# A fused attention and routed-FFN kernel: VectorE's small operations taken from a list, one behind each two-bank maximum

## The chip, the cores and the metric

One core of a Trainium2 chip runs the whole kernel in one launch. The metric is the device time of that launch in microseconds (us). Engines are called TensorE (PE in the profile, its weight loads PEld), VectorE (DVE), ScalarE (ACT), GpSimd (POOL) and SyncE (SP); SP issues most of the DMAs.

## What is computed

The reference takes x (2048 tokens of 512 features) and mixes two branches with a gate per token. Branch a is softmax attention with 32 heads of 16 features. Branch b routes only the two tokens with the highest router score through a SwiGLU feed-forward net; all others pass unchanged.

```python
g = sigmoid((x * gate_w).sum(-1, keepdims=True))
# branch a: 32 heads, Dh = 16
p = softmax(einsum("bhqd,bhkd->bhqk", q, k) * Dh ** -0.5)
a = einsum("bhqk,bhkd->bhqd", p, v) ... @ wo
# branch b: r = x @ w_r; idx = the two largest of r
y = (silu(x_sel @ w_gate) * (x_sel @ w_up)) @ w_down
y = y * sigmoid(r[idx])
b = x + scatter(y at idx)
out = g * a + (1 - g) * b
```

## The kernel before

The attention is cut into 32 units (a pair of heads and half of the queries; the last four are cut otherwise), each of 16 steps (one tile of 128 keys). Everything runs in the order in which the program is written: each engine takes its instructions in that order, and the loops at the end of the function interleave several streams by hand.

Three streams make up the main phase. The **m stream** (`m_piece`, L563) computes scores with queries on the partitions only to find the row maxima of the softmax: 64 matmuls of 512 keys for a unit. Three pieces make a period: two matmuls into the two banks of the tile `mxa`, one into the bank `mxb`. VectorE reduces `mxa` in one instruction (the **two-bank maximum**) and `mxb` in another (the **one-bank maximum**), both at L577, with a minus sign, into `Mr`. The **s stream** (`s_piece`, L634) computes the scores again with keys on the partitions, and ScalarE takes their exponential (L642) into `P`; the negative maximum is in the query operand as two more rows (48 and 49 of each half), so that the exponential needs no bias. The **A stream** (`av_mm`, L644) multiplies `P` with V; a column of ones gives the softmax denominators. The s stream trails the m stream by 21 steps.

The string `ORDER` (L30) sets how they interleave: a round is twelve s, twelve m, three A and one `f`, that is three steps and four periods. `f` is a fill: a quarter of a projection of a later head group, a part of the feed-forward net or of the output projection (`slots`, L800). Work with a due step is entered with `at_step(s, f, ...)` and called by `end_step(s)`, right behind the fourth s piece of step s, wherever VectorE's stream stands then.

Besides the maxima VectorE has small operations:

- the **minimum** (`m_unit`, L614, instruction at L616): when a unit's 64 pieces are reduced, the four partial (negative) maxima of each row are combined. GpSimd then splits the result in a high and a low part (`pool_split`, L75 to L77).
- the **turning** (`m_rows`, L624, instruction at L627): a transpose of 32x32 blocks of the split values, followed by eight DMAs on SP that put them into the two rows of the query tile. The list `turn` holds it together with a count; each maximum takes one off, and at zero, three maxima after the minimum, it is issued.
- the **reciprocals of the denominators** (`l_out`, L691, instruction at L694): eight of 16 columns after every eighth unit, one at the end of each of eight successive steps; the eighth stores them to DRAM on SP.
- the **router**: `route_rows` (L334) takes the eight largest of 16 rows of 128 scores and their places, `route_best` (L344) the eight largest of the 128 candidates; their results go through DMAs on SP. `route_index` and `gather` (L350, L354) fetch the two tokens with indirect DMAs of GpSimd; at the end of `gather` the router's sigmoid is computed, an exponential on ScalarE, "+1" and reciprocal on VectorE. `x_rows` (L362) is the first that uses the fetched tokens.
- the reciprocals of the gates (`gates`, L320) and of the feed-forward's SiLU (`ff_h`, L416).

Of the kernel before, what the change touches and what calls it, by code (L numbers as in the profile page):

```python
# [1 line left out]

# [8 lines left out]
AF = mybir.ActivationFunctionType  # L11
OP = mybir.AluOpType
# [7 lines left out]
UNITS = PAIRS * 2  # L20
# [4 lines left out]
EL = 64  # L25
# [10 lines left out]
def gated_mix(ctx: ExitStack, tc: tile.TileContext, xT, x, wqkv, wo, w_rg, w_gate, w_up, w_down,  # L36
              consts, pos, out):
    nc = tc.nc
# [49 lines left out]
    top8 = cp.tile([16, 8], F32, name="top8")  # L88
    idx8 = cp.tile([16, 8], U32, name="idx8")
    num8 = cp.tile([16, 8], F32, name="num8")  # L90
    cand = cp.tile([1, 128], F32, name="cand")
    best8 = cp.tile([1, 8], F32, name="best8")
# [4 lines left out]
    rsel = cp.tile([2, 1], F32, name="rsel")  # L97
# [202 lines left out]
    rg = {}  # L300
# [32 lines left out]

    def route_rows():  # L334

        nc.vector.max(top8, rg["row"])
        nc.vector.max_index(idx8, top8, rg["row"])
        nc.gpsimd.tensor_copy(num8, idx8)
        nc.gpsimd.tensor_scalar(num8, num8, row0[:16], None, op0=OP.add)
        nc.gpsimd.tensor_copy(idx8, num8)  # L340
        nc.sync.dma_start(cand, top8)
        nc.sync.dma_start(ap(i_scr, 0, [[8, 16], [1, 8]]), idx8)

    def route_best():  # L344
        nc.vector.max(best8, cand)
        nc.vector.max_index(pos8, best8, cand)
        nc.sync.dma_start(pos2, pos8[:, 0:2])
        nc.sync.dma_start(rsel, best8[:, 0:2])
# [5 lines left out]
    def gather():  # L354
        nc.gpsimd.indirect_dma_start(out=xsel, out_offset=None, in_=x,
                                     in_offset=bass.IndirectOffsetOnAxis(ap=idx2[:, :1], axis=0))
        nc.gpsimd.memset(xselT, 0.0)
        nc.scalar.activation(rsel, rsel, AF.Exp, scale=-1.0)
        nc.vector.tensor_scalar(rsel, rsel, 1.0, None, op0=OP.add)
        nc.vector.reciprocal(rsel, rsel)  # L360

    def x_rows():  # L362
        ps = fl_tile((128, 4, 2))
# [199 lines left out]
    def m_piece(g):  # L563

        u, e = divmod(g, EL)
        t, c, j = e // 8, e // 2 % 4, e % 2
        r = g % 3
        if r == 0:
            MX[0] = mxa_tile()
        elif r == 2:  # L570
            MX[1] = mxb_tile()
        dst = MX[0][:, r] if r < 2 else MX[1]
        nc.tensor.matmul(dst, Qx[u % 3][64 * j:64 * j + 48, t * 128:t * 128 + 128],  # L573
                         k_of(u, t // 4)[64 * j:64 * j + 48, c * 512:c * 512 + 512], start=True, stop=True)
        if r:
            g0 = (g - 1 if r == 1 else g) % (3 * EL)
            nc.vector.tensor_reduce(Mr[:, g0:g0 + (2 if r == 1 else 1)], MX[r - 1], axis=AX.X, op=OP.max, negate=True)  # L577
            if turn:
                turn[0][0] -= 1
            if e == EL - 1 or (e == 0 and r == 1 and g):  # L580
                m_unit(u if e else u - 1)
            if turn and turn[0][0] <= 0:
                m_rows(*turn.pop()[1:])

    def m_lead(n):

        if n < 16:
            u, t, c = 0, n // 8 * 4 + n % 4, n // 4 % 2 * 2
        else:
            u, t, c = 1, (n - 16) // 2, n % 2 * 2  # L590
        for i in range(3):
            if i == 0:
                tl = mxa_tile()
                dst = [tl[:, 0], tl[:, 1]]
            else:
                tl = (mxb_tile, fl_tile, av_tile)[(2 * n + i) % 3]()
                dst = [tl]
            for k, d in enumerate(dst):
                j, cc = (k, c) if i == 0 else (i - 1, c + 1)
                nc.tensor.matmul(d, Qx[u][64 * j:64 * j + 48, t * 128:t * 128 + 128],  # L600
                                 Kx[0][64 * j:64 * j + 48, cc * 512:cc * 512 + 512], start=True, stop=True)
            o = EL * u + t * 8 + (c * 2 if i == 0 else c * 2 + 1 + i)
            reds.append((Mr[:, o:o + len(dst)], tl))
        for r in reds:
            nc.vector.tensor_reduce(*r, axis=AX.X, op=OP.max, negate=True)  # L605
        reds.clear()
        if n == 15:
            m_unit(0)
        elif n == 16:
            m_rows(*turn.pop()[1:])  # L610

    reds = []

    def m_unit(u):  # L614
        m = ring.tile([128, 2, 8], F32, tag="m", name="m", bufs=2)
        nc.vector.tensor_reduce(m, Mr[:, EL * (u % 3):EL * (u % 3) + EL].rearrange("p (t c j) -> p j t c", c=4, j=2),  # L616
                                axis=AX.X, op=OP.min)
        hl = ring.tile([128, 2, 2, 8], F32R, tag="hl", name="hl", bufs=2)
        pool_split(hl[:, :, 0], hl[:, :, 1], m)
        turn.append([3 if u < UNITS - 1 else 0, u, hl])  # L620

    turn = []

    def m_rows(u, hl):  # L624

        r = ring.tile([128, 32], F32R, tag="hr", name="hr", bufs=2)
        nc.vector.transpose(r.bitcast(F32), hl.rearrange("p j i t -> p (j i t)").bitcast(F32))  # L627
        for j in range(2):
            for b in range(4):
                q = Qx[u % 3][64 * j + 48:64 * j + 50, :].rearrange("i (t n) -> i t n", n=128)  # L630
                p0 = 32 * b + 16 * j
                nc.sync.dma_start(q[:, :, 32 * b:32 * b + 32].bitcast(F32), r[p0:p0 + 16, :].bitcast(F32))
# [130 lines left out]
    fill, now = {}, [0]  # L763

    def at_step(s, f, *a):
        fill.setdefault(s, []).append((f, a))
# [11 lines left out]
        at_step(-19 + t, products, t)  # L778
    at_step(-1, r_row)
    at_step(1, gates, 0)  # L780
    at_step(2, route_rows)
    at_step(4, gates, 1)
    at_step(10, route_best)
    at_step(16, route_index)
    at_step(22, gather)
    at_step(-8, load_w, 1)
    at_step(-5, split_w, 1)
    at_step(2, load_w, 2)
# [11 lines left out]
    def slots():  # L800
        for w, nb in order:
            yield from proj(1, w, nb, 3)
        late.append((split_w, (2,)))
        at_step(now[0] + 4, load_w, 3)
        x_rows()
        yield
        for w, nb in order:
            yield from proj(2, w, nb, 3)
        for n, (w, nb) in enumerate(order):
            yield from proj(3, w, nb, 3)  # L810
            if w == "q":
                for i in range(4):
                    at_step(now[0] + i + 1, load_ff, ("gate", "up")[i // 2], (w_gate, w_up)[i // 2],
                            ("xh", "xl")[i // 2], nb, i % 2)
        yield from ff_in("gate")
        for j in range(4):
            at_step(now[0] + 2 * j, load_down, j)
        ff_t(0, "gate")
        yield
        yield from ff_in("up")  # L820
        ff_t(1, "up")
        late.append((ff_act, ()))
        at_step(now[0] + 3, ff_h)
        at_step(now[0] + 3, load_wo)
        for c in range(4):
            at_step(now[0] + 6 + c, split_wo, c)
        yield
        yield
        yield from ff_down()
        ff_sum()  # L830
        last_tiles()
        s = now[0]
        for nb in range(4):
            at_step(s + 5 + 2 * nb, load_acc, nb)
        for t in range(16):
            at_step(s + 11 + t, acc_scale, t)
        at_step(s + 1, load_at, 0, (0, 1))
        at_step(s + 4, split_at, 0, (0, 1))
        yield from wait(s + 8)
        yield from wo_groups((0, 1), (2,))  # L840
        assert now[0] > 3 * 8 * KT + 16
        yield from wo_groups((2,))
        for t in range(12, 16):
            wo_last(t, 64)
            yield
        for t in range(12):
            if t % 4 == 0:
                yield from wait((478, 494, 505)[t // 4])
            wo_last(t, 128)
            yield  # L850

    fills = slots()
# [5 lines left out]
    def p_v(s):  # L858
        if not 0 <= s < STEPS:
            return  # L860
        av_mm(s)
        if s % KT < KT - 1:
            return
        u, s = s // KT, now[0]
        av_out(u)
        if u % 8 == 7 and u < 24:
            for i in range(8):
                at_step(s + 6 + i, l_out, u // 8, i)
        elif u == QU - 1:
            for i in range(8):  # L870
                at_step(s + 6 + i, l_out, 3, i)
            for i in range(4):
                at_step(s + 16 + 2 * i, l_last, i // 2, i % 2)
                at_step(s + 19 + 2 * i, n_last, i // 2, i % 2)
            at_step(s + 27, split_last, 3)
        elif QU <= u < UNITS - 1:
            at_step(s + 3, l_unit, u, 0)
            at_step(s + 6, l_unit, u, 1)
            at_step(s + (13 if u == QU else 7), split_last, u - QU)
# [59 lines left out]
        next(fills, None)  # L939
        end_step(s)  # L940
    end_step(STEPS + 2)
    assert next(parts, 0) == 0 and not fill and next(fills, 0) == 0, fill
    tail()


# [29 lines left out]
```

## Time and profile before

| what | value |
|---|---|
| device time, median of 3 runs | 1437.01 us (1435.02 to 1437.27) |
| device time of the profiled execution | 1437.04 us |
| its span, first to last instruction | 1435.2 us |
| TensorE busy | 1423.6 us (99%) |
| VectorE busy | 1295.4 us (90%), 1535 instructions |
| ScalarE busy | 1169.7 us (82%) |
| GpSimd busy | 312.0 us (22%) |
| two-bank maxima (L577) | 655, mean 1213 ns |
| one-bank maxima (L577) | 654, mean 691 ns |

A row of a group reads: line, engine, operation, output and input tiles with their shapes, count, busy time and mean of one, and behind the second bar the idle time of the engine just ahead of these instructions and what ended most of it. A row of a timeline reads: start, duration, engine, line, operation, tiles, and in brackets the idle time ahead and what ended it. Matmuls are pipelined and the ends of their rows are modelled, so their starts are the better measure.

### The profile page before, as it was taken

The numbers are of one execution on the slowest core, as the hardware profiler recorded it, in microseconds if no ns is written. First come the engines' busy times: TensorE is split into PE (matmuls) and PEld (weight loads), VectorE is DVE, ScalarE is ACT, GpSimd is POOL, SyncE is SP. The second block draws the span as 40 slices with busy tenths as digits, with TensorE's granted clock in tenths as the row PEclk, the third lists the DMA queues.
The fourth block names the chain that finished last, engine by engine and source line by source line (L and its number), as shares of the span: only waits on it lengthen the run. The fifth ranks groups of instructions, "written<-read, shape, count | busy, mean of one in ns | idle before, by whom it ended". The sixth has DMA issues, their size and how long they took to land.

```text
span 1435.2 us, 24154 instructions
## 1 busy us (share of the span) xinstructions
PE 1423.6 (99%) x9113; PEld 630.2 (44%) x9113; DVE 1295.4 (90%) x1535; ACT 1169.7 (82%) x2262; POOL 312.0 (22%) x328
## 2 busy tenths in 40 slices
PE   9999999999999999999999999999999999999998
PEld 6654444444444444444444444344444444444433
DVE  5879999999999999999999999999999999999942
ACT  4568888888888888888888888888888888888885
POOL 3652000112000001200000100032742322234500
PEclk9999999999999999999999999999999999999998
DMA  8612021212214121312222332414313031012012
GB/s 266 185 33 63 20 53 31 53 45 40 54 50 112 62 53 30 68 29 57 65 82 53 87 87 73 108 41 128 82 31 68 23 75 37 13 30 58 16 50 77
DMA packets 55096, 92.87 MB, mean 65 GB/s; under 512 B 14208, under 2 KB 25472, under 8 KB 53476
## 3 DMA queue, kind: packets, MB, share of 16 engines
q1 hardware_dynamic: 54884, 91.32, 24.3%
q8 instruction: 72, 1.18, 0.4%
q14 instruction: 44, 0.36, 0.1%
q0 software_dynamic: 96, 0.01, 0.0%
HBM read 63.77 MB, written 28.57 MB: 64 GB/s over the span
## 4 chain that ended last, share of the span: by engine, by line
PE 96%; DMA 2%; DVE 1%; ACT 0%; SPq 0%; issue 0%; ACTq 0%; DVEq 0%
PE av L650 35%; PE st L641 23%; PE mxa L573 12%; PE mxb L573 10%; PE fl L153 6%; PE fl L495 4%; PE st L282 3%; DMA xs<-xT 1%; PE mxa L600 1%; DMA wvs<-wqkv 1%; PE fl L386 0%; PE st L153 0%; DVE Mr L577 0%; DMA k_scr<-Qx 0%; ACT P L642 0%; PE fl L424 0%
## 5 line engine op out<-in xcount | busy, mean ns | idle before, releaser
L642 ACT ACTIVATE P<-st 128x512 f32<-128x512 f32 x2028 | 1064.5, 599 | 204.2 <-PE st L641 102.3
L577 DVE TENSOR_REDUCE Mr<-mxa 128x2 f32<-128x1024 f32 x655 | 794.4, 1213 | 4.0 <-PE mxa L573 3.5
L650 PE MATMUL av<-P,V 128*32 128x512 f32 x4096 | 545.3, 604 | 0.0
L641 PE MATMUL st<-Qx,Kx 50*128 50x512 f32 x2028 | 537.8, 443 | 1.8 <-ACT P L642 1.7
L577 DVE TENSOR_REDUCE Mr<-mxb 128x1 f32<-128x512 f32 x654 | 451.8, 691 | 63.5 <-PE st L641 18.6
L641 PEld LDWEIGHTS st<-Qx,Kx 50*128 50x128 f32 x2028 | 275.3, 184 | 232.7 <-ACT P L642 213.0
L573 PE MATMUL mxb<-Kx,Qx 48*128 48x512 f32 x654 | 325.4, 498 | 0.0
L573 PE MATMUL mxa<-Kx,Qx 48*128 48x512 f32 x1310 | 296.9, 420 | 1.2 <-DVE Mr L577 1.2
L573 PEld LDWEIGHTS mxb<-Kx,Qx 48*128 48x128 f32 x654 | 119.5, 183 | 273.7 <-DVE Mr L577 251.9
L573 PEld LDWEIGHTS mxa<-Kx,Qx 48*128 48x128 f32 x1310 | 124.9, 183 | 52.1 <-DVE Mr L577 9.9
L650 PEld LDWEIGHTS av<-P,V 128*32 128x32 f32 x4096 | 81.1, 108 | 140.6 <-issue 134.5
L189 POOL TENSOR_SCALAR ev<-pe 128x512 fp32r<-128x512 f32 x24 | 35.7, 1489 | 321.5 <-ACT pe L187 321.5
L76 POOL TENSOR_SCALAR hl<-m 128x16 fp32r<-128x16 f32 x32 | 8.1, 254 | 440.0 <-DVE m L616 440.0
L462 POOL TENSOR_TENSOR acc<-acc,w 128x512 f32<-128x512 f32 x32 | 41.0, 1280 | 166.9 <-ACT w L461 152.8
L153 PE MATMUL fl<-xh,wh 128*128 128x512 f32 x96 | 42.9, 447 | 0.0
L153 PE MATMUL fl<-xh,wl 128*128 128x512 f32 x96 | 40.4, 420 | 0.0
L546 DVE SCALAR_TENSOR_TENSOR acc<-fl,gg,acc 128x512 f32<-128x512 f32 x16 | 12.0, 748 | 26.3 <-PE fl L495 24.0
L495 PE MATMUL fl<-woh,ahl 128*128 128x512 f32 x96 | 35.2, 447 | 0.0
L605 DVE TENSOR_REDUCE Mr<-mxa 128x2 f32<-128x1024 f32 x21 | 25.7, 1222 | 8.3 <-PE mxa L600 8.3
L153 PE MATMUL fl<-xl,wh 128*128 128x512 f32 x96 | 32.6, 421 | 0.0
L190 POOL TENSOR_TENSOR ev<-pe,ev 128x512 fp32r<-128x512 f32 x24 | 30.8, 1283 | 2.0
L282 PE MATMUL st<-Kx,xh 128*128 128x512 f32 x64 | 28.1, 440 | 0.0
(173 smaller groups left out, 763.0 us busy)
## 6 DMA issues: line engine op xcount, KB each, us to landing
Kx<-k_scr SPq DMA_DIRECT2D x30, 256.0 KB
k_scr<-ev SPq DMA_DIRECT2D x14, 512.0 KB
q_scr<-ev SPq DMA_DIRECT2D x14, 512.0 KB
Qx<-q_scr SPq DMA_DIRECT2D x54, 128.0 KB
Qx<-q_scr SPq DMA_DIRECT2D x70, 64.0 KB
xs<-xT SPq DMA_DIRECT2D x16, 256.0 KB
xn<-x SPq DMA_DIRECT2D x4, 1024.0 KB
Qx<-hr SPq DMA_DIRECT2D x256, 2.0 KB
```

Source lines behind the costliest of these rows:

```text
L153: nc.tensor.matmul(ps, a[:, i, c, :], b[nb][:, c, :], start=n == 0, stop=n == 11)
L189: nc.gpsimd.tensor_scalar(ev[:, 0], t, 1.0, None, op0=OP.mult)
L190: nc.gpsimd.tensor_sub(ev[:, 1], t, ev[:, 0].bitcast(F32))
L282: nc.tensor.matmul(ps, a[nb][:, c, sl], b[:, c, :], start=c == 0 and n == 0, stop=c == 3 and n == 2)
L462: nc.gpsimd.tensor_add(a, a, w)
L495: nc.tensor.matmul(ps, a[:, sl], b[:a.shape[0], c, :], start=first and n == 0, stop=last and n == 2)
L573: nc.tensor.matmul(dst, Qx[u % 3][64 * j:64 * j + 48, t * 128:t * 128 + 128], k_of(u, t // 4)[64 * j:64 * j + 48, c * 512:c * 512 + 512], ...
L577: nc.vector.tensor_reduce(Mr[:, g0:g0 + (2 if r == 1 else 1)], MX[r - 1], axis=AX.X, op=OP.max, negate=True)
L605: nc.vector.tensor_reduce(*r, axis=AX.X, op=OP.max, negate=True)
L641: nc.tensor.matmul(ps, k, q, start=True, stop=True)
L642: nc.scalar.activation(P[s][:, 2 * j + c, :], ps, AF.Exp)
L650: nc.tensor.matmul(AV[0][32 * ct:32 * ct + 32, :], V[:, kt, h * VW:h * VW + 32], P[s][:, ct, :], start=kt == 0, stop=kt == KT - 1)
```

## The change

A list `gaps` holds closures. In `m_piece`, directly behind a two-bank maximum (r == 1), a pending turning is issued if there is one; otherwise, if the piece isn't among the first two or the last of its unit, the oldest entry of `gaps` is called. So at most one of them follows each two-bank maximum. The count in `turn` is gone: the turning of a unit follows the first two-bank maximum after its minimum. `m_unit`, which issues the minimum, is called where it was: behind a two-bank maximum in two of three units, behind a one-bank maximum in the third.

The denominators' reciprocals, the router's two pairs, the gates' reciprocal and `ff_h` no longer run at the end of a step but are appended to `gaps` there. Each of the router's pairs is taken apart, the MAX8 one entry and the rest another. Some due steps are later by one or two (`route_best` 10 to 12, `route_index` 16 to 18, `gather` 22 to 24). The router's sigmoid becomes a function of its own: the exponential stays at step 22, its "+1" goes from VectorE to GpSimd, and its reciprocal is appended at step 27.

```diff
@@ route_rows, route_best, gather
-        nc.vector.max(top8, rg["row"])
         nc.vector.max_index(idx8, top8, rg["row"])
-        nc.vector.max(best8, cand)
         nc.vector.max_index(pos8, best8, cand)
-        nc.scalar.activation(rsel, rsel, AF.Exp, scale=-1.0)
-        nc.vector.tensor_scalar(rsel, rsel, 1.0, None, op0=OP.add)
-        nc.vector.reciprocal(rsel, rsel)
+    def route_gate(i):
+        if i == 0:
+            nc.scalar.activation(rsel, rsel, AF.Exp, scale=-1.0)
+            nc.gpsimd.tensor_scalar(rsel, rsel, 1.0, None, op0=OP.add)
+        else:
+            nc.vector.reciprocal(rsel, rsel)
@@ m_piece
             nc.vector.tensor_reduce(Mr[:, g0:g0 + (2 if r == 1 else 1)], MX[r - 1], axis=AX.X, op=OP.max, negate=True)
-            if turn:
-                turn[0][0] -= 1
+            if r == 1:
+                if turn:
+                    m_rows(*turn.pop())
+                elif e > 1 and e < EL - 1 and gaps:
+                    gaps.pop(0)()
             if e == EL - 1 or (e == 0 and r == 1 and g):
                 m_unit(u if e else u - 1)
-            if turn and turn[0][0] <= 0:
-                m_rows(*turn.pop()[1:])
+                if u == UNITS - 1 and e:
+                    m_rows(*turn.pop())
@@ m_unit
-        turn.append([3 if u < UNITS - 1 else 0, u, hl])
+        turn.append((u, hl))
-    turn = []
+    turn, gaps = [], []
@@ due steps
-    at_step(2, route_rows)
-    at_step(4, gates, 1)
-    at_step(10, route_best)
-    at_step(16, route_index)
-    at_step(22, gather)
+    at_step(2, gaps.append, lambda: nc.vector.max(top8, rg["row"]))
+    at_step(3, gaps.append, route_rows)
+    at_step(4, gaps.append, partial(gates, 1))
+    at_step(10, gaps.append, lambda: nc.vector.max(best8, cand))
+    at_step(12, gaps.append, route_best)
+    at_step(18, route_index)
+    at_step(22, route_gate, 0)
+    at_step(24, gather)
+    at_step(27, gaps.append, partial(route_gate, 1))
-        at_step(now[0] + 3, ff_h)
+        at_step(now[0] + 3, gaps.append, ff_h)
-                at_step(s + 6 + i, l_out, u // 8, i)
+                at_step(s + 6 + i, gaps.append, partial(l_out, u // 8, i))
-                at_step(s + 6 + i, l_out, 3, i)
+                at_step(s + 6 + i, gaps.append, partial(l_out, 3, i))
```

More of the change, by code (lines that the diff above doesn't have):

```diff
@@ L1 @@
 from contextlib import ExitStack
+from functools import partial
 import concourse.bass as bass
@@ L609, in m_lead @@
         elif n == 16:
-            m_rows(*turn.pop()[1:])
+            m_rows(*turn.pop())
     reds = []
@@ L941, in gated_mix @@
     end_step(STEPS + 2)
-    assert next(parts, 0) == 0 and not fill and next(fills, 0) == 0, fill
+    assert next(parts, 0) == 0 and not gaps and not fill and next(fills, 0) == 0, fill
     tail()
```

## The prediction

> **What bounds the kernel now.** I read the page first (busy time, chain), then the groups by line, the waits, and last the timeline of VectorE and of TensorE, one engine at a time, because the change only shifts VectorE's small operations by a few instructions.
>
> ```profile
> span 1435.2 us, 24154 instructions
> ...
> PE 1423.6 (99%) x9113; PEld 630.2 (44%) x9113; DVE 1295.4 (90%) x1535; ACT 1169.7 (82%) x2262; POOL 312.0 (22%) x328
> ...
> PE 96%; DMA 2%; DVE 1%; ACT 0%; SPq 0%; issue 0%; ACTq 0%; DVEq 0%
> ...
> L577 DVE TENSOR_REDUCE Mr<-mxa 128x2 f32<-128x1024 f32 x655 | 794.4, 1213 | 4.0 <-PE mxa L573 3.5
> ...
> L577 DVE TENSOR_REDUCE Mr<-mxb 128x1 f32<-128x512 f32 x654 | 451.8, 691 | 63.5 <-PE st L641 18.6
> ```
>
> TensorE is busy for 1423.6 us of 1435.2 and has 96% of the chain that ended last; VectorE follows at 90%. A two-bank and a one-bank maximum take 1213 + 691 = 1904 ns together, so VectorE has little room in a period (one of each). Ahead of a two-bank maximum it idles 4.0 us in all, ahead of a one-bank maximum 63.5 us, or 97 ns each: VectorE's spare time lies behind the two-bank maximum. Four undisturbed periods show both engines:
>
> ```profile
> 402.91 1.21 DVE L577 TENSOR_REDUCE Mr<-mxa 128x2 f32<-128x1024 f32 x1
> 404.22 0.69 DVE L577 TENSOR_REDUCE Mr<-mxb 128x1 f32<-128x512 f32 x1
> 404.83 1.22 DVE L577 TENSOR_REDUCE Mr<-mxa 128x2 f32<-128x1024 f32 x1
> 406.16 0.69 DVE L577 TENSOR_REDUCE Mr<-mxb 128x1 f32<-128x512 f32 x1
> 406.76 1.22 DVE L577 TENSOR_REDUCE Mr<-mxa 128x2 f32<-128x1024 f32 x1
> 408.00 0.69 DVE L577 TENSOR_REDUCE Mr<-mxb 128x1 f32<-128x512 f32 x1
> 408.61 1.22 DVE L577 TENSOR_REDUCE Mr<-mxa 128x2 f32<-128x1024 f32 x1
> 410.02 0.69 DVE L577 TENSOR_REDUCE Mr<-mxb 128x1 f32<-128x512 f32 x1 [0.20 <-PE st L641]
> ```
> ```profile
> 404.24 0.46 PE L573 MATMUL mxa<-Kx,Qx 48*128 48x512 f32 x2
> ...
> 406.19 0.41 PE L573 MATMUL mxa<-Kx,Qx 48*128 48x512 f32 x2
> ...
> 408.04 0.52 PE L573 MATMUL mxa<-Kx,Qx 48*128 48x512 f32 x2
> ...
> 410.06 0.39 PE L573 MATMUL mxa<-Kx,Qx 48*128 48x512 f32 x2
> ```
>
> A period is about 1.9 us (402.91, 404.83, 406.76, 408.61). From a one-bank maximum to the two-bank one is 0.61 us, back to back. From a two-bank to the next one-bank maximum it is 1.31, 1.33, 1.24 and 1.41 us, mean 1.32: the last part is waiting for TensorE. The two-bank maxima end at 404.12, 406.05, 407.98 and 409.83, and the score matmuls that overwrite their banks start 0.12, 0.14, 0.06 and 0.23 us later. Where TensorE really waits (below), it starts about 0.06 us after the end, so the **slack** of a two-bank maximum is 0.06, 0.08, 0 and 0.17 us, mean 0.08. Whatever delays it by more stops TensorE, and TensorE is the chain. A delay of a one-bank maximum first eats up the gap in front of it.
>
> **The change part by part.** It removes one operation of VectorE and moves the others. The matmuls keep their order, and so do ScalarE's activations.
>
> *Router.* Three groups stand behind one-bank maxima today.
>
> ```profile
> 104.41 0.27 DVE L336 MAX8 top<-rt 16x8 f32<-16x128 f32 x1
> 104.71 0.08 DVE L337 MATCH_VALUE_LOAD idx<-top,rt 16x8 f32 x1
> ...
> 104.99 1.19 DVE L577 TENSOR_REDUCE Mr<-mxa 128x2 f32<-128x1024 f32 x1
> ```
> ```profile
> 106.24 0.50 PE L573 MATMUL mxa<-Kx,Qx 48*128 48x512 f32 x2 [0.35 <-DVE Mr L577]
> ```
> ```profile
> 126.20 0.27 DVE L345 MAX8 best<-cand 1x8 f32<-1x128 f32 x1
> ...
> 126.78 1.19 DVE L577 TENSOR_REDUCE Mr<-mxa 128x2 f32<-128x1024 f32 x1
> ```
> ```profile
> 128.08 0.50 PE L573 MATMUL mxa<-Kx,Qx 48*128 48x512 f32 x2 [0.33 <-DVE Mr L577]
> ```
> ```profile
> 157.15 0.69 DVE L577 TENSOR_REDUCE Mr<-mxb 128x1 f32<-128x512 f32 x1
> 158.37 0.14 DVE L359 TENSOR_SCALAR rsel<-rsel 2x1 f32<-2x1 f32 x1 [0.53 <-ACT rsel L358]
> ...
> 158.62 1.19 DVE L577 TENSOR_REDUCE Mr<-mxa 128x2 f32<-128x1024 f32 x1
> ```
> ```profile
> 159.87 0.50 PE L573 MATMUL mxa<-Kx,Qx 48*128 48x512 f32 x2 [0.51 <-DVE Mr L577]
> ```
>
> At 104.41 stood a MAX8 and a FIND_INDEX8 (with its value load). Without them the two-bank maximum would have ended at 104.41 + 1.21 = 105.62; it ended at 104.99 + 1.19 = 106.18, 0.56 us late, and TensorE shows 0.35 us idle, ended by that maximum. The same pair at 126.20: end at 127.97 instead of 127.41, 0.56 late, 0.33 idle. At 158.37 VectorE waited 0.53 us for ScalarE's exponential and then ran two tiny operations: the maximum ended at 159.81 instead of 157.15 + 0.61 + 1.21 = 158.97, 0.84 late, 0.51 idle. The visible idle, 0.35 + 0.33 + 0.51 = 1.19 us, is a lower bound, the whole delay, 1.96 us, an upper one. I take delay less mean slack: 0.48 + 0.48 + 0.76 = **1.72 us**.
>
> What is late next: MAX8, FIND_INDEX8 and the reciprocals now stand singly in gaps. From FIND_INDEX8's load to the next maximum is 104.99 - 104.71 = 0.28 us; in a gap it would start 1.13 us after the two-bank maximum (shown below), and 1.13 + 0.28 = 1.41 is 0.09 more than the mean gap, against 0.08 of slack: nothing, twice. The "+1" of the router's gate goes to GpSimd, which is idle then; ScalarE is no longer waited for by VectorE, since the reciprocal is queued five steps later. On SP, two weight loads now go ahead of the candidates' store, and eight row loads ahead of the store of the positions: a few microseconds, while TensorE first uses the gathered rows at 352.3 us, so I cost this at nothing.
>
> ```profile
> L365 PE MATMUL fl<-cst,xsel x4: 196/197/218, 352.3 to 352.5; 2*128 2x2 f32 x4
> ```
>
> Were that cover gone, VectorE's second MAX8 would wait for the candidates. Elsewhere on SP one feed-forward weight load changes places with a store of denominators, also far from its use.
>
> *Softmax denominators.* Of 32 reciprocals (4 bursts of 8), by the order of VectorE's instructions, 21 stand behind a one-bank maximum and 11 behind a two-bank one; all 32 go into gaps.
>
> ```profile
> L627 DVE STREAM_TRANSPOSE hr<-hl 128x32 f32<-128x32 f32 x32 | 6.4, 201 | 0.7 <-POOL hl L77 0.7
> L694 DVE RECIPROCAL Lt<-Lt 128x16 f32<-128x16 f32 x24 | 5.8, 241 | 0.0
> ```
> ```profile
> 780.71 0.24 DVE L694 RECIPROCAL Lt<-Lt 128x16 f32<-128x16 f32 x1
> 780.87 1.16 DVE L577 TENSOR_REDUCE Mr<-mxa 128x2 f32<-128x1024 f32 x1
> ...
> 782.73 1.21 DVE L577 TENSOR_REDUCE Mr<-mxa 128x2 f32<-128x1024 f32 x1
> 783.86 0.24 DVE L694 RECIPROCAL Lt<-Lt 128x16 f32<-128x16 f32 x1
> ...
> 791.92 0.24 DVE L694 RECIPROCAL Lt<-Lt 128x16 f32<-128x16 f32 x1
> 792.08 0.63 DVE L577 TENSOR_REDUCE Mr<-mxb 128x1 f32<-128x512 f32 x1
> ```
>
> Behind a one-bank maximum (780.71): the next maximum starts 0.16 us later but takes 1.16 instead of 1.21, so it ends 0.11 late; less 0.08 of slack, 0.03 us, and 21 x 0.03 = **0.63 us** (between 0 and 21 x 0.11 = 2.3; I stay near the slack because the slack is read from four rows of this stage). In a gap (783.86) it starts 1.13 us after the two-bank maximum; the next maximum can follow 0.16 us later (791.92 to 792.08): 1.29 of the mean 1.32 us. So a reciprocal in a gap costs nothing on average; in the tightest place of four (1.24) the one-bank maximum is 0.05 us late, which is under the mean slack. A burst of eight still runs within the period: 0.61 + 1.29 = 1.90.
>
> *Turnings* (32 transposes, 201 ns). Twenty leave a one-bank maximum for a gap. A transpose is shorter than a reciprocal, so it gains 0 to 0.03 us each: I take 0.01, **0.2 us**. Their eight row loads on SP go out up to 2 us sooner, behind the same neighbours.
>
> *Minima.* The edit leaves their call where it is: ten of 32 remain behind a one-bank maximum. But there the turning now follows the very next two-bank maximum, which is already late; its gap is used up, so I charge 10 x 0.02 = **-0.2 us** (between 0 and 10 x 0.11). Whether the operand is ready:
>
> ```profile
> 294.62 1.20 DVE L577 TENSOR_REDUCE Mr<-mxa 128x2 f32<-128x1024 f32 x1
> ```
> ```profile
> 295.12 0.22 POOL L77 TENSOR_TENSOR hl<-m,hl 128x16 fp32r<-128x16 f32 x1
> ```
> ```profile
> 419.32 1.49 POOL L189 TENSOR_SCALAR ev<-pe 128x512 fp32r<-128x512 f32 x1
> ```
>
> GpSimd's second half ends at 295.34, and VectorE would ask at 294.62 + 1.20 = 295.82: 0.48 us ahead. The new wait ends first, if GpSimd is free.
>
> *Gate and feed-forward reciprocals*: two of the same kind, +0.1 us; *tight gaps* of MAX8 and the rest, -0.05 us.
>
> Sum: 1.72 + 0.63 + 0.2 - 0.2 + 0.1 - 0.05 = **2.4 us**. The profiled execution took 1437.04 us (span 1435.2 and 1.84 around it), within 0.03 of the median shown, 1437.01. Forecast: 1437.04 - 2.4 = **1434.6 us**, 0.17% less.
>
> **Rivals.** *Order is indifferent*: VectorE's sum of work sets the pace, and only the removed "+1" counts, 0.14 us by its row: 1436.9. For it speaks that VectorE is 90% busy; against it the 0.35, 0.33 and 0.51 us of TensorE's idle at three places where operations stood behind a one-bank maximum. The Trainium skill, "VectorE: DVE Perf Modes", section "Rules for kernel authors", speaks this way against the change: "Minimize op *count*, not sems", since the pipeline is flushed after each operation wherever it stands. By that rule the sum would be 0.14 us; the trace agrees only partly, since the reciprocal at 783.86 began 0.08 us before the reported end of the maximum ahead of it.
>
> *The gap is not free*: if every one of some 70 operations in gaps costs what it would in the tightest place (0.05 us), that is -3.5 us against 2.65 of gains: 1437.9. The mean gap speaks against it, the bursts (five in consecutive gaps) for it.
>
> *Slower*: the turning waits for GpSimd. In the ten units above it is asked for 0.48 us after the split ends. At 419.32 a 1.49 us operation of GpSimd starts just behind such a split. If one came in front, the split would end 1.0 us after VectorE asks, VectorE would stand, and less gap and slack each costs some 0.8 us: 8 us, 1442.6. It decides from the point at which GpSimd's queue delays the split by 0.5 us. Against it: GpSimd's queue keeps its order there.
>
> **How the numbers follow.** Forecast 0.74, order indifferent 0.12, gap not free 0.09, slower mechanism 0.05. The forecast's own spread: up, the whole delay of the router (1.96) and reciprocals at 0.08 (1.7), a gain of 3.6, 1433.4; down, the visible idle alone with the gap's costs, about 1 us, 1436. The range takes in the indifferent case and the spread of the runs (1437.27): **1433.4 to 1437.3**. About 0.2%, 2.9 us, is what a measurement of this kernel can tell from no change: faster means under 1434.1, which the upper part of my forecast reaches: 0.30. Slower means above 1439.9: 0.05. Within: 0.65.
>
> **What would show it.** TensorE's idle ended by the two-bank maximum (now three waits) is gone; the idle ahead of one-bank maxima falls by about what the moved operations take; the 32 reciprocals stand behind two-bank maxima with the next score matmul on time; ten minima still delay theirs. I am wrong if transposes show waits for GpSimd's split, if score matmuls come late behind the bursts, or if the three idles vanish and the time stays.

## The result and the profile after

The changed kernel takes 1432.39 us (median of nine runs, 1430.75 to 1435.03) against 1436.64 us before (nine runs, 1435.02 to 1439.03): the ratio is 0.9969, with a 95% interval of 0.9961 to 0.9978, so 3.2 to 5.6 us less. That is faster by 0.3%, and outside the stated range (1433.4 to 1437.3). A later kernel with the same order of instructions (the control below, ten runs) gave 1433.84 against 1436.51, ratio 0.9984 (0.9974 to 0.9993), so 1.0 to 3.7 us less. The two intervals share a gain of 3.2 to 3.7 us.

The profiled execution took 1430.75 us. Its page shows the same picture as before: TensorE carries the chain, VectorE is at 90%.

```profile
span 1428.9 us, 24152 instructions
...
PE 1417.6 (99%) x9113; PEld 628.9 (44%) x9113; DVE 1292.6 (90%) x1534; ACT 1169.4 (82%) x2262; POOL 312.9 (22%) x329
...
PE 97%; DMA 2%; SPq 0%; DVE 0%; ACT 0%; issue 0%; ACTq 0%; DVEq 0%
...
L580 DVE TENSOR_REDUCE Mr<-mxa 128x2 f32<-128x1024 f32 x655 | 796.6, 1216 | 3.9 <-PE mxa L576 3.0
...
L580 DVE TENSOR_REDUCE Mr<-mxb 128x1 f32<-128x512 f32 x654 | 450.9, 689 | 62.6 <-PE st L648 20.6
```

The prediction expected the idle ahead of one-bank maxima to fall by about what the moved operations take. It fell only from 63.5 to 62.6 us, though 48 more operations stand in those gaps (21 reciprocals of denominators, 20 turnings, 7 of the router, the gates and the feed-forward), and VectorE's busy time fell by 2.8 us (1295.4 to 1292.6). Part of their time lies beside the end of the maximum ahead of them (a reciprocal in a gap starts 1.13 us after the start of a maximum of 1.21); where the rest went was not measured. The row that moved is TensorE's waiting for two-bank maxima. The waits view (us in total, times, longest) of the kernel before, whose three waits of a matmul (second row) were the router's places:

```profile
PEld mxa L573 <- DVE Mr L577: 9.9, 38, 0.8
...
PE mxa L573 <- DVE Mr L577: 1.2, 3, 0.5
```

and of the changed kernel, where that second row is gone:

```profile
PEld mxa L576 <- DVE Mr L580: 5.4, 21, 0.3
...
DVE hr L634 <- POOL hl L78: 0.7, 1, 0.7
```

The transposes' only wait for GpSimd's split (last row) is the 0.7 us of the first unit, as before. At the router's first place a MAX8 now stands in the gap, and the score matmul starts 0.10 us after the end of the maximum ahead of it (104.29 + 1.22 = 105.51):

```profile
104.29 1.22 DVE L580 TENSOR_REDUCE Mr<-mxa 128x2 f32<-128x1024 f32 x1
105.42 0.27 DVE L788 MAX8 top<-rt 16x8 f32<-16x128 f32 x1
```
```profile
105.61 0.45 PE L576 MATMUL mxa<-Kx,Qx 48*128 48x512 f32 x2
```

**Where the time went.** Two-bank maxima run through the whole main phase, so the view of their line gives its length: start of the first to start of the last (duration minimum/median/maximum in ns, then the two starts). Before, after, and the kernel before profiled once more:

```profile
L577 DVE TENSOR_REDUCE Mr<-mxa x655: 1152/1215/1227, 95.3 to 1368.9; 128x2 f32<-128x1024 f32 x164
```
```profile
L580 DVE TENSOR_REDUCE Mr<-mxa x655: 1164/1215/1228, 95.2 to 1364.9; 128x2 f32<-128x1024 f32 x164
```
```profile
L577 DVE TENSOR_REDUCE Mr<-mxa x655: 1151/1216/1227, 98.0 to 1371.0; 128x2 f32<-128x1024 f32 x164
```

This stretch is 1273.6 us before, 1269.7 after, 1273.0 in the repeat: 3.3 to 3.9 us less. Laying the starts of the score matmuls of both traces over each other, the difference hardly moves for hundreds of microseconds and jumps at the changed places: 1.9 us at the router's three, 1.1 us at the four bursts (their turnings included), about 0.5 to 0.7 us, depending on which profile of before is taken, at the turnings of the other units whose minimum stands in a gap, and nothing that stands out of the repeat's noise at those that follow a late minimum.

Behind the stretch both kernels run the same instructions for the same 51.9 us up to the last attention matmul. Then the profiles differ again. Shown are the copy of the last attention output and the view of all that follows it (PEclk, the mean granted clock of TensorE, is the last column but two), first of the kernel before, then of the changed one:

```profile
1421.50 0.60 ACT L663 ACTIVATE o<-av 128x512 f32<-128x512 f32 x1 [1.21 <-PE av L650]
```
```profile
1421.50:1435.25 13.75, 8.19 (x28) 6.27 (x28) 5.10 (x10) 1.84 (x4) 0.00 (x0) 0.71 0.20 76
```
```profile
1417.49 0.60 ACT L670 ACTIVATE o<-av 128x512 f32<-128x512 f32 x1 [1.21 <-PE av L657]
```
```profile
1417.49:1428.93 11.44, 5.46 (x28) 4.11 (x28) 4.92 (x10) 1.76 (x4) 0.00 (x0) 1.00 0.24 92
```

From that copy to the end of the span (the **tail**) it is 13.75 us before and 11.44 after, with a mean granted clock of 0.71 and 1.00. TensorE runs the same 28 matmuls there, and nothing of the change is in the tail; its clock varies from run to run (below). So of the 6.3 us between the two spans some 2.3 are the tail's clock in those two executions, and 3.9 the stretch of maxima.

### The profile page after: what moved, and what is told of

Read it like the earlier page. It is cut to its first block, busy times and chain, and to the rows that moved or that the text cites. A ratio compares the mean times of both kernels' runs of the same rounds, so it can differ in the third digit from the quotient of the medians.

```text
span 1428.9 us, 24152 instructions
## 1 busy us (share of the span) xinstructions
PE 1417.6 (99%) x9113; PEld 628.9 (44%) x9113; DVE 1292.6 (90%) x1534; ACT 1169.4 (82%) x2262; POOL 312.9 (22%) x329
## 4 chain that ended last, share of the span: by engine, by line
PE 97%; DMA 2%; SPq 0%; DVE 0%; ACT 0%; issue 0%; ACTq 0%; DVEq 0%
PE av L657 36%; PE st L648 24%; PE mxa L576 12%; PE mxb L576 10%; PE fl L154 6%; PE fl L498 4%; PE st L283 3%; DMA xs<-xT 1%; PE mxa L607 1%; DMA wvs<-wqkv 1%; PE fl L389 0%; PE st L154 0%; DMA k_scr<-Qx 0%; PE fl L427 0%; ACT P L649 0%; DVE acc L549 0%
## 5 line engine op out<-in xcount | busy, mean ns | idle before, releaser
L580 DVE TENSOR_REDUCE Mr<-mxb 128x1 f32<-128x512 f32 x654 | 450.9, 689 | 62.6 <-PE st L648 20.6
L319 ACT ACTIVATE p<-p 128x512 f32<-128x512 f32 x32 | 20.0, 628 | 11.1 <-POOL p L315 10.9
```

## The experiments

**Each part alone.** Three kernels, each the kernel before with one part of the change. The stretch of maxima is the measure, since the times of single runs of one kernel spread over 2 to 4 us. The stretch itself differs by 0.6 us between the two profiles of before, so what a part gives is read from the jumps of the matmul starts at its own places.

The router's part, with the reciprocal of the gates (lines of the edit; `...` stands for others):

```diff
+            if r == 1 and e > 1 and e < EL - 1 and gaps:
+                gaps.pop(0)()
...
-    at_step(2, route_rows)
...
+    at_step(2, gaps.append, lambda: nc.vector.max(top8, rg["row"]))
+    at_step(3, gaps.append, route_rows)
...
-        nc.vector.tensor_scalar(rsel, rsel, 1.0, None, op0=OP.add)
+            nc.gpsimd.tensor_scalar(rsel, rsel, 1.0, None, op0=OP.add)
```

> The kernel before with the router's part alone (its operations, the gates' and the router's reciprocal in the list, the +1 on GpSimd); reciprocals of the denominators, turnings and ff_h as before. By late maxima (a late two-bank maximum stops TensorE): the stretch from the first to the last L577 maximum, 1273.6 us before, falls by 1.9 us, as the staircase of score-matmul starts between the two traces has it; the sum of the prediction says 1.7. By order indifferent: 0.1 us.

```profile
L580 DVE TENSOR_REDUCE Mr<-mxa x655: 1152/1214/1227, 97.8 to 1369.5; 128x2 f32<-128x1024 f32 x164
```

1271.7 us: 1.9 less than the first profile of before, 1.3 less than the second; at the three places themselves the matmul starts gain 1.9 us against either. Time 1436.17 against 1436.70, ratio 0.9995 (0.9986 to 1.0005), which alone would settle nothing. *Order is indifferent* (0.1 us) falls.

The reciprocals of the denominators (with the same two lines that call the list):

```diff
-                at_step(s + 6 + i, l_out, u // 8, i)
+                at_step(s + 6 + i, gaps.append, partial(l_out, u // 8, i))
```

> The kernel before with the 32 denominators' reciprocals alone in the list. By late maxima: the stretch of maxima falls by 1.0 us, in four steps at the four bursts; by the prediction's size 0.6 us; by order indifferent 0; if a gap is not free, it grows by up to 1 us.

```profile
L578 DVE TENSOR_REDUCE Mr<-mxa x655: 1159/1214/1227, 95.5 to 1368.2; 128x2 f32<-128x1024 f32 x164
```

1272.7 us: 0.9 and 0.3 less than the two profiles of before; at the four bursts alone 0.9 to 1.0 us. Time ratio 0.9994 (0.9985 to 1.0004).

The turnings:

```diff
-            if turn:
-                turn[0][0] -= 1
+            if r == 1 and turn:
+                m_rows(*turn.pop()[1:])
...
-            if turn and turn[0][0] <= 0:
-                m_rows(*turn.pop()[1:])
```

> The kernel before with the turnings alone moved behind the next two-bank maximum. By the two traces' difference what is left for the turnings is 0.9 us, some 0.03 us for each unit; the prediction's own terms (plus 0.2, minus 0.2) give 0; if turnings wait for GpSimd's split, it grows by up to 8 us. Order indifferent: 0.

```profile
L577 DVE TENSOR_REDUCE Mr<-mxa x655: 1152/1214/1228, 95.3 to 1367.9; 128x2 f32<-128x1024 f32 x164
```

1272.6 us: 1.0 and 0.4 less than the two. At the units' ends alone (those in bursts and behind late minima left out) it is about 0.5 to 0.7 us, most of it in the ten units whose turnings stood at one place of the round. Time ratio 0.9996 (0.9986 to 1.0005). A wait for GpSimd, up to 8 us, didn't come. Measured at their own places, the three parts add up to 1.9 + 1.0 + 0.5 to 0.7 = 3.4 to 3.6 us, against 3.3 to 3.9 for the change as a whole.

**Same list, other side.** Is it the gap that matters, or that the operations are issued one at a time?

```diff
             if r == 1:
                 if turn:
                     m_rows(*turn.pop())
-                elif e > 1 and e < EL - 1 and gaps:
-                    gaps.pop(0)()
+            elif e > 1 and e < EL - 1 and gaps:
+                gaps.pop(0)()
```

> The changed kernel with the list emptied behind one-bank maxima instead of two-bank ones; turnings as in the changed kernel. By late maxima: the 32 reciprocals cost 1.0 x 32 / 21 = 1.6 us and the router's single operations some 0.7 us more than in the changed kernel, so the stretch of maxima is 2 us longer than its 1269.7. By order indifferent, or if the gain came from taking the operations one at a time: the same as the changed kernel.

```profile
L580 DVE TENSOR_REDUCE Mr<-mxa x655: 1152/1214/1227, 95.4 to 1366.7; 128x2 f32<-128x1024 f32 x164
```

1271.3 us, 1.6 more than the changed kernel, a little under the expected 2. At the bursts nothing of the 1.1 us is left: there it is the gap that counts. At the router's places 1.6 of 1.9 us remain: there the gain came mostly from taking the pairs apart and from no longer waiting for ScalarE, not from the gap. Which of these two gave how much was not tested. Time 1434.67, ratio 0.9983 (0.9974 to 0.9993).

**The place in the round.** The prediction subtracted one mean slack, 0.08 us, from every delay. In the quiet periods of before, those without a small operation near, the slack is not spread at random: its mean is 0.00, 0.15, 0.06 and 0.08 us at the four places of a round (ends of the maxima to starts of the matmuls, 0.06 us of the way from one to the other taken off). The four rows of the prediction had the same order, 0, 0.17, 0.06 and 0.08. Two kernels put 24 reciprocals back behind one-bank maxima, once at the roomiest place and once at the tightest, and a control has only the second buffer that these need (last two lines). The edit of the roomy place; that of the tight one has `== 1` in place of `== 2`:

```diff
+            elif g // 3 % 4 == 2 and e > 1 and e < EL - 1 and ones_bank:
+                ones_bank.pop(0)()
...
-                at_step(s + 6 + i, gaps.append, partial(l_out, u // 8, i))
+                at_step(s + 6 + i, ones_bank.append, partial(l_out, u // 8, i))
...
-            Lt[g] = ring.tile([128, 128], F32, tag="Lt", name="Lt", bufs=1)
+            Lt[g] = ring.tile([128, 128], F32, tag="Lt", name="Lt", bufs=2)
```

> The changed kernel with 24 of the 32 reciprocals put back behind one-bank maxima, but only one in a round of four periods and at that place of the round where the next two-bank maximum has most slack (0.15 us; a second buffer for the denominators gives the time for it). A reciprocal there delays by 0.11 us. If the cost is delay less the slack of the place: nothing, the stretch of maxima as in the changed kernel (within 0.3 us). If a mean slack of 0.08 us counts, as the prediction's sum had it: 24 x 0.03 = 0.7 us longer. If every operation behind a one-bank maximum delays TensorE: 24 x 0.11 = 2.6 us longer.

> The same 24 reciprocals at the place of the round where the next two-bank maximum has no slack. By the slack of the place: 24 x 0.11 = 2.6 us longer than in the changed kernel. By a mean slack: 0.7 us longer, as at the other place. By order indifferent: the same as the changed kernel.

> The changed kernel with the second buffer for the denominators alone, as the measure for the other two on the same chip. The stretch of maxima is 1269.7 us within 0.3, the time that of the changed kernel, about 4 us less than before.

The stretches of the roomy place, the tight place and the control, in this order:

```profile
L580 DVE TENSOR_REDUCE Mr<-mxa x655: 1159/1215/1227, 96.7 to 1367.2; 128x2 f32<-128x1024 f32 x164
```
```profile
L580 DVE TENSOR_REDUCE Mr<-mxa x655: 1159/1215/1228, 95.0 to 1366.8; 128x2 f32<-128x1024 f32 x164
```
```profile
L580 DVE TENSOR_REDUCE Mr<-mxa x655: 1160/1215/1227, 95.3 to 1365.2; 128x2 f32<-128x1024 f32 x164
```

The control's stretch is 1269.9 us, the roomy place's 1270.5, the tight place's 1271.8. So 24 reciprocals cost 0.6 us (0.03 each) at the one and 1.9 us (0.08 each) at the other, for the same instruction behind the same kind of maximum. The 0.6 us alone would be no more than two profiles of one kernel differ by; but at the three bursts themselves the matmul starts lose 0.5 us and 2.1 us against the control. The first reciprocal of each shows it, first VectorE's and then TensorE's timeline of the roomy kernel:

```profile
454.20 0.24 DVE L703 RECIPROCAL Lt<-Lt 128x16 f32<-128x16 f32 x1
454.36 1.16 DVE L580 TENSOR_REDUCE Mr<-mxa 128x2 f32<-128x1024 f32 x1
```
```profile
455.63 0.44 PE L576 MATMUL mxa<-Kx,Qx 48*128 48x512 f32 x2
```

and of the tight one:

```profile
450.61 0.24 DVE L703 RECIPROCAL Lt<-Lt 128x16 f32<-128x16 f32 x1
450.77 1.16 DVE L580 TENSOR_REDUCE Mr<-mxa 128x2 f32<-128x1024 f32 x1
```
```profile
451.99 0.50 PE L576 MATMUL mxa<-Kx,Qx 48*128 48x512 f32 x2
```

In the first the late maximum ends at 455.52 and the matmul starts 0.11 us later; it was not waiting. In the second the maximum ends at 451.93 and the matmul starts 0.06 us later, as it does wherever TensorE waits. Neither count was met: the roomy place wasn't quite free (0.6 us is what the mean slack gives), and the tight one cost 0.08 rather than 0.11 us. What is shown is that the place counts, not that its mean slack gives the exact price. Times 1433.60, 1434.54 and 1433.84, ratios 0.9982 (0.9972 to 0.9992), 0.9990 (0.9980 to 0.9999) and 0.9984 (0.9974 to 0.9993): the times don't separate the three, the stretches do. The control's time is 2.7 us under before, where about 4 were expected.

**The minima that stayed.** The ten minima behind one-bank maxima were left alone by the change. In the changed kernel's VectorE timeline, and TensorE's matmul behind it:

```profile
291.42 0.69 DVE L580 TENSOR_REDUCE Mr<-mxb 128x1 f32<-128x512 f32 x1 [0.18 <-PE mxb L576]
292.15 0.22 DVE L623 TENSOR_REDUCE m<-Mr 128x16 f32<-128x64 f32 x1
292.30 1.20 DVE L580 TENSOR_REDUCE Mr<-mxa 128x2 f32<-128x1024 f32 x1
293.43 0.19 DVE L634 STREAM_TRANSPOSE hr<-hl 128x32 f32<-128x32 f32 x1
293.55 0.64 DVE L580 TENSOR_REDUCE Mr<-mxb 128x1 f32<-128x512 f32 x1
```
```profile
293.56 0.50 PE L576 MATMUL mxa<-Kx,Qx 48*128 48x512 f32 x2
```

The minimum begins 0.73 us after the start of the one-bank maximum, where another operation begins 0.61 after it, and the two-bank maximum begins 0.88 us after that same start. It ends at 293.50, and the matmul starts 0.06 us later. The minimum is late because it reads what that maximum wrote: in the same trace the 20 minima behind a two-bank maximum whose result they read start 1.25 to 1.26 us after its start, and the turnings and reciprocals there, which don't read it, 1.13 to 1.14. The next kernel holds these minima for the next gap as well, and the turning for the one after:

```diff
             if r == 1:
                 if turn:
                     m_rows(*turn.pop())
+                elif unit:
+                    m_unit(unit.pop())
...
+            if e == EL - 1 and r == 2:
+                unit.append(u)
-            if e == EL - 1 or (e == 0 and r == 1 and g):
+            elif e == EL - 1 or (e == 0 and r == 1 and g):
```

> The changed kernel with the ten minima that stand behind a one-bank maximum also held for the next two-bank one (the turning then one further). By late maxima: each of the ten costs 0.2 us today in the periods around it, so the stretch of maxima falls by 2.0 us from 1269.7 to 1267.7, and the time to about 1430.4. By order indifferent, or if a minimum delays TensorE through what waits for it: no change.

```profile
L580 DVE TENSOR_REDUCE Mr<-mxa x655: 1159/1215/1227, 95.4 to 1363.2; 128x2 f32<-128x1024 f32 x164
```
```profile
292.01 1.22 DVE L580 TENSOR_REDUCE Mr<-mxa 128x2 f32<-128x1024 f32 x1
293.14 0.21 DVE L627 TENSOR_REDUCE m<-Mr 128x16 f32<-128x64 f32 x1
293.45 0.69 DVE L580 TENSOR_REDUCE Mr<-mxb 128x1 f32<-128x512 f32 x1
```

1267.8 us, 1.9 less than the changed kernel, as expected (2.0). The minimum now follows a two-bank maximum whose result it doesn't read, and starts 1.13 us after the start of that one, like a reciprocal there. Time 1430.81 against 1436.27, ratio 0.9956 (0.9943 to 0.9970).

**What the runs' spread is.**

> The kernel before once more. By late maxima its stretch of maxima (1273.6 us) repeats within 0.1 us, and the spread of the times, some 2 to 4 us, lies ahead of it and behind it: if the granted clock's low stretches fall on the tail at random, runs at a mean clock of 0.998 are some 1 to 2 us faster than runs at 0.996. If the main phase itself varies, the stretch differs by a microsecond or more.

The stretch repeated within 0.6 us (1273.0), not 0.1. Eleven runs gave 1434.31 to 1438.09 us (ratio to before 1.0001, 0.9992 to 1.0010). The one run at a mean clock of 0.999 was the fastest (1434.31), the three slowest (1437.82 to 1438.09) were at 0.996; but the other three at 0.996 gave 1436.44 to 1436.50, among the four at 0.998 with 1436.42 to 1436.95. So the mean clock of a run goes with its time only in part.

The thirteen profiles of this document show where the spread lies. From the copy of the last attention output to the end it is 11.4 to 11.5 us in the four in which the granted clock stayed full until TensorE's last matmul (the changed kernel, the roomy place and the two with extra matmuls below), 12.3 to 13.0 in the five with one stretch of 3.41 us at half clock before that matmul, and 13.7 to 13.9 in the four with one of 6.83 us. And the part ahead of the main phase varies by more: the first two-bank maximum starts between 95.0 and 98.0 us. The profile of the repeat has a shorter tail than the first one of before (12.6 us), and yet a longer span (1436.3 us), because its main phase starts 2.7 us later (98.0 instead of 95.3). What sets that start was not looked into.

To test whether the tail's low clock comes from TensorE's idling there, a kernel got nine matmuls more, into a bank that nothing reads, in three places of the tail (3 ahead of the matmuls that gather the last denominators, 4 behind them, 2 behind those that spread the reciprocals):

```diff
+        def warmer(n):
+            for _ in range(n):
+                nc.tensor.matmul(mx[:, 1], wz[0][:, 0, :128], wz[0][:, 0, :], start=True, stop=True)
...
+        warmer(3)
...
+        warmer(4)
...
+        warmer(2)
```

> The changed kernel with nine matmuls into an unused bank in the tail's three waits of TensorE (their result is not used). If the tail's length hangs on the granted clock falling to half when TensorE idles there: the clock stays at 1 to the end, the tail (from the copy of the last attention output on) is 11 us or less in every run, and the median falls by 1 to 2 us and the spread shrinks. If the low clock is not caused by that idling: no change, or up to 1 us slower by the added matmuls.

> Minima in gaps and the tail's extra matmuls together, on the changed kernel. If both theories hold, 2.0 + 1 to 2 us less than the changed kernel: about 1429. If only the minima count, 1430.4.

The tail of the kernel with the minima alone, and of the one with minima and extra matmuls (both on the same chip), the copy of the last output and all that follows it:

```profile
1415.75 0.60 ACT L674 ACTIVATE o<-av 128x512 f32<-128x512 f32 x1 [1.21 <-PE av L661]
```
```profile
1415.75:1429.46 13.71, 8.16 (x28) 6.23 (x28) 5.10 (x10) 1.84 (x4) 0.00 (x0) 0.70 0.20 77
```
```profile
1415.11 0.60 ACT L674 ACTIVATE o<-av 128x512 f32<-128x512 f32 x1 [1.21 <-PE av L661]
```
```profile
1415.11:1426.55 11.44, 7.44 (x37) 5.28 (x37) 4.92 (x10) 1.76 (x4) 0.00 (x0) 1.00 0.24 92
```

From the copy to the end it is 13.71 us at a mean clock of 0.70, and 11.44 us at 1.00, though with nine matmuls more (11 us or less was expected). All five runs with both had a mean clock of 0.999, the five with the minima alone 0.996 or 0.997. The times follow less clearly: 1429.94 us (1428.18 to 1430.10) with both, ratio 0.9950 (0.9937 to 0.9964), against 1430.81 (1429.91 to 1431.26); about 1429 was expected if both parts count, 1430.4 if the minima alone do. The extra matmuls on the changed kernel alone gave 1431.46 (1430.04 to 1432.17), ratio 0.9962 (0.9948 to 0.9975), with mean clocks of 0.998 and 0.999; the interval overlaps that of the changed kernel. So it is shown that the tail's length hangs on the clock, and that the clock stayed up in both profiles with extra matmuls, against two of the eleven without. That this makes the median 1 to 2 us shorter is not shown. The kernel with both has the lowest median, 6.3 us less than before; its interval overlaps that of the minima alone.

## Why the prediction was wrong

- **Mechanism and sign were right, the sizes were not.** A two-bank maximum that is late by more than its slack stops TensorE; the router's pairs and the reciprocals stopped it, and in the changed kernel they don't. *Order is indifferent*, *the gap is not free* and *the turning waits for GpSimd* all fell (the same list on the other side cost 1.6 us; with 48 more operations in gaps the waits of the weight loads fell from 38 to 21; the only wait for the split is an old one). For the router the prediction gave the gap too much credit: single operations behind one-bank maxima keep 1.6 of the 1.9 us.
- **The step that failed** is the mean slack of 0.08 us, taken off every delay whatever place of the round it stands at. The next three terms rest on it, wholly or in part.
- **Reciprocals, 0.63 us**: measured 0.9 to 1.0. The step is "less 0.08 of slack, 0.03 us, and 21 x 0.03". Ten of the 21 stood at the place of the round without slack, eleven at the one with 0.15 us: 10 x (0.11 - 0) + 11 x 0 = 1.1. A mean over four rows hides that a place with room can't give its room to the next one. The two kernels with 24 reciprocals at one place each show the difference (0.08 against 0.03 us each).
- **Router, 1.72 us**: measured 1.9. At the three places the matmul starts jump by 0.55, 0.57 and 0.76 us, where the sum had 0.48, 0.48 and 0.76. The first two gave nearly their whole delay of 0.56. The pair at 126.20 stood at the place without slack. The one at 104.41 stood at the place with 0.15 us on average, but in that very period there was little room: in the changed kernel the matmul starts 0.10 us after the maximum's end, 0.04 us of slack. The gate's wait stood at the place without slack; its 0.84 us jumped by 0.84 and fell back to 0.76 a period later.
- **Turnings, 0.2 us, and the charge of 0.2 us behind late minima**: measured about 0.5 to 0.7 together, forecast 0. Ten of the twenty turnings stood at the place with 0.06 us of slack, ten at that with 0.15. A two-bank maximum behind one ends 0.09 us late (it runs from 255.76 to 256.94 in the kernel before; back to back it would have ended at 256.85), which by place gives 10 x 0.03 = 0.3 us. So the mean slack accounts for a part; where the rest comes from is not shown. And the charge was not there: at 293.43 the turning follows a late two-bank maximum, yet the next pair of score matmuls starts 2.00 us after the late one, as it did before without the turning (293.56 to 295.56, and 295.88 to 297.88).
- **Gate and feed-forward reciprocals, 0.1 us**: at neither place do the matmul starts move by more than 0.01 us.
- **Minima left behind one-bank maxima**: rightly seen to stay; their price, 0.19 us each, was not worked out, and is the largest single remainder.
- **Sum, 2.4 us**: the main phase gave 3.3 to 3.9. Router, reciprocals and turnings were all put too low.
- **The starting point and the range.** The forecast was counted from 1437.04 us; nine runs of before had a median of 1436.64. And the tail adds 0 to 2.3 us with the clock of the moment, and the part ahead of the main phase up to 3 us, a spread that the range had at its upper end alone (the 1437.27 of one run) and not at its lower end. With 3.3 to 3.9 us from 1436.64 the change stands at about 1433, just under the range. The 1432.39 probably has some luck with the clock in it: seven of its nine runs had a mean clock of 0.998 or 0.999, against three of ten of the control, which took 1433.84.
- The Trainium skill, "VectorE: DVE Perf Modes", section "Rules for kernel authors", has the rule that the prediction cites ("Minimize op *count*, not sems"). By it the change was worth 0.14 us. The trace does not agree: with one operation fewer of 1535, the main phase became 3.3 to 3.9 us shorter.

## What to carry to other kernels

Where two engines take turns on a buffer in a fixed round, list the slack of each place of the round, and price an inserted operation as delay less slack at its own place, with nothing below zero; only then add up. Here this came closer than a mean slack, but not exact. Put small operations of the second engine where it waits anyway, one at a time, and look for those that read what the instruction just ahead of them wrote, since they start later still. When the effect is smaller than the spread of whole runs, measure the stretch that the change touches.

## What the runs showed of the hardware

- A small operation of VectorE that doesn't read the previous result starts 1.13 to 1.14 us after the start of a two-bank maximum of 1.21 to 1.22 us, before its reported end; a minimum that reads it starts 1.25 to 1.26 us after (changed kernel). Behind a one-bank maximum it is 0.59 to 0.61 us without that dependence (turnings of the kernel before) and 0.72 to 0.73 with it.
- The clock granted to TensorE fell to half in stretches of 3.41 us or twice that in the tail, where TensorE waits for others: 0.70 and 0.71 as the mean from the last copy to the end in two profiles, and 13.7 against 11.4 us for that part. Where it falls varies between runs of one kernel. With nine idle-filling matmuls it didn't fall before TensorE's last matmul in the two profiles taken. The Trainium skill, "TensorE: Matmul & The Clock Gate", section "Part 1: The HAM clock gate (the "warmup" mystery)", states such windows (about 3.4 us, half clock after one idle window). The trace agrees with the length and the half. But in the tail TensorE was busy for 0.54 to 0.65 of the 3.41 us ahead of such a drop (nine profiles), and how much idling is enough no run here shows.
